# Free-list buffers, a DMA channel and TensorE's pace in a planner's model, and new tables, in an attention, convolution and expert kernel

## The chip, the cores and the metric

The kernel runs on one core of one Trainium2 chip. Its parts are TensorE (PE, matrix products; PEld is its load of stationary operands), VectorE (DVE), ScalarE (ACT), GpSimd (POOL) and SyncE (SP), which only issues transfers here, together with 16 DMA engines. The metric is the device time of one execution in microseconds (us).

## The reference

Three things are computed one after the other. Attention: 8 batches, 8 heads, 256 positions, 64 features per head. Then a gated convolution of 15 taps along the sequence, separately for each of the 512 features, with a silu, added to the attention's output. Then a mixture of experts with two levels of choice (4 groups of 4 experts), where each of the 2048 tokens goes through the one expert that wins.

```python
attn = softmax(q @ k.T / sqrt(D)); x = attn @ v            # B=8 H=8 S=256 D=64, as (B, S, 512)
x_g = x * sigmoid(glu_gate)
conv_out = sum over k of x_g[s + k - 7] * conv_w[:, k]      # 15 taps
x = x + conv_out * sigmoid(conv_out)
g = argmax(x @ w_group); e = argmax(x @ w_expert[g])        # per token
out = softmax weight of g * softmax weight of e * (relu(x @ w1[g, e]) @ w2[g, e])   # 512 -> 1024 -> 512
```

## The kernel before

**Tiles.** A unit `U` is one pair of heads (128 features on the 128 partitions) of two batches; there are 16. Four units, the whole width of 512 features, make a group of two batches (`GS = 2, 2, 2, 2`), and there are four groups. A large operation works on a tile of 128 x 512.

**A unit's way.** `inputs` issues its two loads, qk and gv, on SP's queue. `unit` scales the keys (L327), turns the gate into a tanh (L338) and adds one (t1, L343 or L345). `pair` and `head` do the attention: scores (L362), row maximum on VectorE (`reduce_max`, L390), exponential on ScalarE (L395), transposes on TensorE (L402), a copy pT out of PSUM, the product with v (L381). `tail` builds the reciprocal sums (rb, rc), multiplies (L445, the unit's xT) and gates it (xg, L453). `conv` runs the 15 taps on VectorE (L513, L515), one instruction of 128 x 512 each; for units 2 and 3 (`PC`) `conv_pe` does them as matrix products. Silu and `residual` close the unit; x is split into a high part xh and a low part xl, so that the expert products run in fp32r with three terms.

**A group's way.** `rows` writes the tokens' rows to memory, `route` finds each token's expert (logits at L608, the last step at L697), and picks for each batch the most frequent expert. `loads` and `split` bring that expert's weights in eight pieces of 512 KB (raw) and split each into wh (a cast, L205) and wl (two subtractions of 128 x 512, L731). `dense` runs the batch through it (L758, then L776 to L778), and `store` scales and writes. Tokens with another expert are gathered into three slots (`leftover`, L939 and L963), whose weights come into the gv buffers. A loop at the end takes what still remains; it does not run with these inputs.

**What sets the order.** All instructions are issued in an order that `Flow` plans before the kernel is built. Every step of a generator names an engine, an assumed duration and a key; when the model's engine becomes free, the step with the lowest key among those that are ready goes next. `KEYS` shifts the key of a kind of step, `CD` that of a group's convolutions, and `WAYS` says, one digit for each time, which of the listed engines takes it. Buffers are rings: `get` waits for the oldest one to be returned with `put`. On the chip, each engine runs its instructions in the planned order and waits where data is late. The plan itself costs no time on the chip.

**Start.** `warm` sends `WN` products of zeros through TensorE before the first data is there (L268). SP's queue begins with half of unit 0's qk, the three constants (c_sb with the identity for transposes, the taps cwq, the router's weights wr), and the other half.

## Time and profile before

| | |
|---|---|
| median of 3 runs | 390.2 us (388.56 to 390.43) |
| profiled execution, its own time | 389.96 us |
| its span, first to last instruction | 388.2 us |
| mean granted TensorE clock | 0.974 of 2.4 GHz |
| busy: PE, DVE, POOL, ACT | 359.3, 298.7, 280.7, 224.3 us |

The span is what the profile shows; some 1.8 us of the execution's time lie outside it. A group of instructions is named by its line in the kernel, its engine and its operation. "Idle" and "waited" are times in which an engine stood still until the instruction named after the arrow had ended. The granted clock is 1.00 at 2.4 GHz and 0.50 at 1.2 GHz.

### The profile page before, as it was taken

To read this page: it belongs to the slowest core of one execution; us is meant where nothing else is said; L and a number is where in the kernel's file an instruction comes from. 1 tells how busy PE (TensorE), PEld (TensorE's weight loads), DVE (VectorE), ACT (ScalarE), POOL (GpSimd) and SP (SyncE) were. 2 spreads that over 40 slices of the span, in tenths; PEclk is the share of its full clock that TensorE was granted. 3 is DMA by queue.
4 is the path that set the end of the run, shared out by engine and by line. 5 is a ranking of instruction groups with operands and counts; after the bars stand their busy time and mean duration, and the time that the engine had idled before them with its cause. 6 is when DMAs were issued, how large, how long until landed. Compare 5 with 4: busy or idle time off the path is not lost.

```text
span 388.2 us, 8398 instructions
## 1 busy us (share of the span) xinstructions
PE 359.3 (93%) x2974; PEld 279.6 (72%) x2974; DVE 298.7 (77%) x590; ACT 224.3 (58%) x525; POOL 280.7 (72%) x273
## 2 busy tenths in 40 slices
PE   8898996879999997999999999999799999998993
PEld 7455543658767776877886768878787987986982
DVE  2389989899999999899999999999855541542630
ACT  2888984688858776776878496502443443431210
POOL 4754668299999997899989785877798566376430
PEclk9899999889999998999999999999899999999998
DMA  7523963276617556262643641388858897958301
GB/s 273 218 109 127 253 178 107 86 268 245 214 50 280 209 171 213 114 218 76 221 144 116 205 164 54 117 289 280 301 209 270 302 363 252 345 196 308 110 0 59
DMA packets 27820, 74.88 MB, mean 193 GB/s; under 512 B 2886, under 2 KB 3014, under 8 KB 27776
## 3 DMA queue, kind: packets, MB, share of 16 engines
q1 hardware_dynamic: 24128, 67.79, 51.3%
q10 hardware_dynamic: 3456, 6.29, 4.3%
q8 instruction: 25, 0.41, 0.4%
q0 software_dynamic: 192, 0.24, 0.2%
q14 instruction: 19, 0.16, 0.1%
HBM read 63.67 MB, written 8.59 MB: 186 GB/s over the span
## 4 chain that ended last, share of the span: by engine, by line
PE 43%; DVE 39%; ACT 7%; issue 4%; DMA 3%; POOL 1%; SPq 1%; ACTq 0%; DVEq 0%; POOLq 0%
DVE ac L515 19%; PE sc L758 11%; DVE nm L390 6%; PE mo L776 4%; PE mo L778 4%; PE mo L777 4%; ACT pr L395 3%; PE sc L362 3%; PE av L381 2%; DVE ac L513 2%; PE sc L402 2%; DVE hl L791 2%; PE mo L758 2%; DVE xT L445 2%; PE mo L268 2%
## 5 line engine op out<-in xcount | busy, mean ns | idle before, releaser
L731 POOL TENSOR_TENSOR wl<-raw,wh 128x512 fp32r<-128x512 f32 x117 | 150.4, 1307 | 36.8 <-ACT wh L205 27.0
L515 DVE SCALAR_TENSOR_TENSOR ac<-xg,cwq,ac 128x512 f32<-128x512 f32 x182 | 133.2, 749 | 2.5
L205 ACT CAST wh<-raw 128x1024 fp32r<-128x1024 f32 x54 | 56.7, 1051 | 25.2 <-PE mo L778 20.0
L395 ACT ACTIVATE pr<-sc,nm 128x256 f32<-128x256 f32 x108 | 50.3, 476 | 33.3 <-DVE nm L390 32.9
L776 PE MATMUL mo<-wh,hh 128*128 128x512 f32 x128 | 53.4, 417 | 0.0
L778 PE MATMUL mo<-wh,hl 128*128 128x512 f32 x128 | 50.3, 393 | 0.0
L777 PE MATMUL mo<-wl,hh 128*128 128x512 f32 x128 | 50.1, 391 | 0.0
L402 PE MATMUL sc<-c_sb,pr 128*128 128x128 f32 x216 | 34.3, 288 | 9.9 <-ACT pr L395 9.7
L381 PE MATMUL av<-pT,gv 128*64 128x256 f32 x256 | 38.4, 401 | 3.1 <-ACT pT L205 3.1
L390 DVE TENSOR_REDUCE nm<-sc 128x2 f32<-128x512 f32 x54 | 34.6, 681 | 6.8 <-PE sc L362 6.6
L402 PEld LDWEIGHTS sc<-c_sb,pr 128*128 128x128 f32 x216 | 25.0, 145 | 20.1 <-ACT pr L395 15.3
L362 PE MATMUL sc<-qk 64*128 64x256 f32 x216 | 32.6, 419 | 0.0
L205 ACT COPY pT<-sc 128x512 f32<-128x512 f32 x52 | 30.0, 598 | 4.6 <-PE sc L402 3.8
L453 POOL TENSOR_TENSOR xg<-xT,gv 128x512 f32<-128x512 f32 x16 | 20.9, 1309 | 15.7 <-DVE xT L445 15.6
L776 PEld LDWEIGHTS mo<-wh,hh 128*128 128x128 f32 x128 | 24.0, 188 | 7.9 <-issue 3.2
L381 PEld LDWEIGHTS av<-pT,gv 128*64 128x64 f32 x256 | 17.0, 139 | 16.4 <-ACT pT L205 7.0
L778 PEld LDWEIGHTS mo<-wh,hl 128*128 128x128 f32 x128 | 24.0, 188 | 5.5
L327 POOL TENSOR_SCALAR qk<-qk 128x512 f32<-128x512 f32 (+1 forms) x16 | 23.0, 1439 | 5.7 <-DMA qk<-aQ 5.7
L777 PEld LDWEIGHTS mo<-wl,hh 128*128 128x128 f32 x128 | 24.1, 189 | 4.0
L789 ACT ACTIVATE hh<-sc 128x512 fp32r<-128x512 f32 x18 | 10.8, 598 | 27.1 <-PE sc L758 23.0
L362 PEld LDWEIGHTS sc<-qk 64*128 64x128 f32 x216 | 20.1, 196 | 8.8 <-issue 5.9
L758 PE MATMUL sc<-xT,wh 128*128 128x256 f32 x144 | 24.6, 289 | 0.0
(207 smaller groups left out, 726.2 us busy)
## 6 DMA issues: line engine op xcount, KB each, us to landing
raw<-wE SPq DMA_DIRECT2D x64, 512.0 KB, 4.5
gv<-wE SPq DMA_DIRECT2D x24, 512.0 KB, 5.9
gv<-aG SPq DMA_DIRECT2D x16, 512.0 KB, 5.6
qk<-aQ SPq DMA_DIRECT2D x15, 512.0 KB, 4.6
x_rows<-y ACTq DMA_DIRECT2D x13, 256.0 KB, 2.8
out_dram<-y ACTq DMA_DIRECT2D x11, 256.0 KB, 3.3
out_dram<-y SPq DMA_DIRECT2D x5, 256.0 KB, 5.0
wh<-xg SPq DMA_DIRECT2D x4, 270.0 KB, 4.7
```

Of the source, the lines that this page charges most:

```text
L205: (a_.copy if e == "ACT" else on[e].tensor_copy)(o, i)
L362: t_.matmul(scs[hh][:, qt, :], t[sl, i, qt * P:(qt + 1) * P], t[sl, i, 256:512], start=True, stop=True)
L381: t_.matmul(u.a[64 * hh:64 * hh + 64, i, :], u.vt[:, i, kt, hh, :], pTs[hh][1][:, kt, :], start=kt == 0, stop=kt == 1)
L390: v_.reduce_max(nm[:, hh, :], sc, axis=AX.X, negate=True)
L395: a_.activation(pr[:, qt, :], sc[:, qt, :], AF.Exp, bias=nm[:, hh, qt:qt + 1], scale=1.0, accum_out=u.sm[:, i, qt, hh, 0:1])
L402: t_.transpose(tp[:, kt, qt * P:(qt + 1) * P], pr[:, qt, kt * P:(kt + 1) * P], ident)
L515: v_.scalar_tensor_tensor(acc if k == KT - 1 else ac, x, w, ac, ALU.mult, ALU.add)
L731: on[e].tensor_tensor(wl[:, sl], raw[:, sl], wh[:, sl].bitcast(F32), ALU.subtract)
L758: t_.matmul(hp[:, f, :], ww[:, f, c, :], x, start=k == 0, stop=k == 11)
L776: t_.matmul(ys[t], hh[:, k, sl], w3h[:, k, :], start=j == 0 and k == 0, stop=False)
L777: t_.matmul(ys[t], hh[:, k, sl], w3l[:, k, :], start=False, stop=False)
L778: t_.matmul(ys[t], hl[:, k, sl], w3h[:, k, :], start=False, stop=j == 3 and k == 1)
```

## The change

The buffers that hold xg, xT, xh and xl (16 and 19 in two rings) become 25 slots of one size in a free list: `take` asks for any free slot, `back` returns it. The first use of a slot for xg is asked for behind the gate's tanh, for xT behind the last product with v. xh and xl are returned behind the first layer of the group's last batch. `NQK` goes from 3 to 2 and `HB`, the buffers of the hidden layer, from 4 to 7.

The plan's model changes: `land` is one DMA channel of 400 KB per us with 2.0 us of latency, where SP was held for 0.9 to 1.8 us per load before; an issue now holds SP for 0.45. `pace` stretches TensorE's steps in the model where it has been idle. Some assumed durations are new.

At the start, 36 products of zeros are sent instead of 61, both halves of unit 0's qk are issued first, then c_sb, and cwq and wr only behind unit 1's loads, with a flag `taps` ahead of the convolutions. `UC`, the products of the first expert layer that are planned as one step, goes from 6 to 4. rb may be made on POOL. `CD`, `KEYS` and `WAYS` are new. Where `WAYS` has a 1 for xg, the step t1 falls away and VectorE adds one and multiplies in one instruction.

```diff
--- before.py
+++ after.py
-WN = 61
+WN = 36
...
-N1, N2 = (NC * GS.count(n) for n in (1, 2))
-XS = 0, 3
-HB = 4
-NQK, NGV = 3, 5
+NSL = 25
+HB = 7
+NQK = 2
+NGV = 5
...
-CD = 4.5, 5.37, 11.11, 14.25
+CD = 9.29, 16.05, 17.59, 10.88
...
-UC = 6
+UC = 4
...
-WAYS = dict(rb='0000000000000001', rc='1', xd='0000001000010001', yd='00000001100111', xr='00000000000011', t1='000001111', wh='000000001000000000000000000000000111100000000000000000000101111', ls='01011', pT='00000000000000000000000000010000000000000000000000000000000001', kk='0000000000001', xh='01000000011001', xl='0000000000100001', silu='000000000000012', res='000001000010101', y='000000110111111', wl='0000000000000000000000000000000000000000000000000000000000000000001000000000000000000000000000000000010101010110000001000010101')
-KEYS = dict(tg=-0.45, tp=0.19, rb=1.65, res=1.05, th=-6.86, ls=1.56, conv=1.51, hl=2.4, wh=3.95, t1=1.96, lt=0.08, cp=-2.0, hh=-1.85, max=0.9, sp=-3.29, xr=-1.54, rows=1.63, exp=0.27, dn=0.24, xl=-0.19, rc=0.35)
+WAYS = dict(xg='00000001000101', kk='100100000011', xh='1100010000111011', ls='111', xr='001', yd='000110011', res='0000010000000101', xd='0011001111100011', rc='10001', t1='1101010101100111', wh='000000000001000010000001001010000010000010000101110111', silu='2112220202200011', pT='101100000000000000000000000000000000000000000000000000010011', xl='01010000000101', y='001001000111111', wl='00000001000000000100000000000000000000000000000001010101000100010101000101100000000000011001000000000000111110101111111010000111', rb='2211000000010022')
+KEYS = dict(av=1.39, rt=17.63, max=-6.26, rows=-10.24, cp=7.78, score=0.71, x=-9.24, exp=-0.24, tg=1.23, rb=0.33, ls=4.81, y=-8.67, xg=0.95, t1=0.43, lt=1.85, rc=-3.04, dn=0.11, tp=0.52, res=1.78, pT=0.07, wh=1.78)
...
+    def pool(self, b, n):
+        self.spare[b], self.want[b] = [(0.0, None, i) for i in range(n)], []
+
+    def serve(self, b):
+        while self.want[b] and self.spare[b]:
+            w = min(self.want[b], key=lambda x: x[:2])
+            self.want[b].remove(w)
+            x = min(self.spare[b], key=lambda x: (x[0], x[2]))
+            self.spare[b].remove(x)
+            k = w[2]
+            if x[0] > k[2]:
+                k[2:4] = x[:2]
+            k[4] = x[2]
+            now = self.now
+            self.step(k)
+            self.now = now
+
+    def back(self, b, i):
+        self.spare[b].append((*self.now[2:4], i))
+        self.serve(b)
+
+    def land(self, kb):
+        self.chan = max(self.now[2] + 2.0, self.chan) + kb / 400
+        return self.chan
+
+    def pace(self, t, d):
+        if t >= self.slow:
+            a = max(0.0, t - 4.0)
+            busy = sum(max(0.0, min(y, t) - max(x, a)) for x, y in self.pe[-12:])
+            if t > 5.0 and busy < 2.3:
+                self.slow = t + 4.0
+        if t < self.slow:
+            d = min(2 * d, d + (self.slow - t) / 2)
+        self.pe.append((t, t + d))
+        return d
...
-            k[2], k[3], k[4] = t + x[3], e, e
+            k[2], k[3], k[4] = t + (self.pace(t, x[3]) if e == "PE" else x[3]), e, e
...
-              hb=HB, y=2, rb=1, xg1=N1, xg2=N2, xT1=N1 + XS[0], xT2=N2 + XS[1])
+              hb=HB, y=2, rb=1)
+    fl.pool("sl", NSL)
...
+    def slot(i, dt, u, w=S):
+        return work.tile([P, MB, XW], dt, name=f"sl{i}", bufs=1)[:, 0:u.nb, 0:w]
...
     def setup():
         s_.dma_start(out=c_sb, in_=cst)
+        fl.go(ready1(), KP, fl.land(420))
+
+    def ready1():
+        yield run("DVE", 0.1, 0.5)
+        v_.tensor_copy(rec[:, :, 0], tok1)
+        v_.memset(base, 0.0)
+
+    taps = Flag()
+
+    def ready2():
+        yield run("DVE", 0.15, -1)
+        v_.tensor_scalar(cwq, cwq, 0.25, None, ALU.mult)
+        fl.set(taps)
+
+    def setup2():
         s_.dma_start(out=cwq, in_=cw)
         s_.dma_start(out=wr_sb, in_=wr)
-        v_.tensor_scalar(cwq, cwq, 0.25, None, ALU.mult)
-        v_.tensor_copy(rec[:, :, 0], tok1)
-        v_.memset(base, 0.0)
+        fl.go(ready2(), KP, fl.land(1000))
...
     def inputs():
-        for u in us:
-            u.ng = yield get(f"xg{u.nb}")
-            u.xg = work.tile([P, u.nb, XW], F32, name=f"xg{u.nb}", bufs=fl.bufs[f"xg{u.nb}"])
-            u.nx = yield get(f"xT{u.nb}")
-            u.xT = work.tile([P, u.nb, S], F32, name=f"xT{u.nb}", bufs=fl.bufs[f"xT{u.nb}"])
         for u in us:
             u.iq = yield get("qk")
             u.qk = inp.tile([P, MB, 512], F32, name="qk", bufs=NQK)
             if u.n == 0:
                 u.half = []
                 for i in range(u.nb):
-                    yield run("SP", 1.0)
+                    yield run("SP", 0.45)
                     s_.dma_start(out=u.qk[:, i], in_=aQ[u.b + i, u.p])
-                    u.half.append(fl.now[2] + 2.0)
-                    if i == 0:
-                        setup()
+                    u.half.append(fl.land(256))
+                yield run("SP", 0.45)
+                setup()
             else:
-                yield run("SP", 0.9 * u.nb)
+                yield run("SP", 0.45)
                 s_.dma_start(out=u.qk[:, 0:u.nb], in_=aQ[u.b:u.b + u.nb, u.p].rearrange("b p f -> p b f"))
-            qt = fl.now[2] + 2.0
+                qt = fl.land(256 * u.nb)
             u.iv = yield get("gv")
             u.gv = inp.tile([P, MB, 512], F32, name="gv", bufs=NGV)
-            yield run("SP", 0.9 * u.nb)
+            yield run("SP", 0.45)
             s_.dma_start(out=u.gv[:, 0:u.nb], in_=aG[u.b:u.b + u.nb, u.p].rearrange("b p f -> p b f"))
-            u.tv = fl.now[2] + 2.0
+            u.tv = fl.land(256 * u.nb)
             fl.go(unit(u), u.k, qt if u.n else u.half[0])
+            if u.n == 1:
+                yield run("SP", 0.9)
+                setup2()
...
-            e = yield at("t1", u.n, KP, ("POOL", 0.1 + 0.57 * nb), ("ACT", 0.1 + 0.21 * nb))
+            e = yield at("t1", u.n, KP, ("POOL", 0.49 * nb), ("ACT", 0.1 + 0.21 * nb))
             if e == "POOL":
                 g_.tensor_tensor(tg, tg, ones[:, 0:1].unsqueeze(1).broadcast_to([P, nb, 256]), ALU.add)
             else:
                 a_.activation(tg, tg, AF.Copy, bias=1.0)
         fl.set(u.gate)
-        yield run("POOL", 0.2, KP)
+        u.ng = yield take("sl")
+        u.xg = slot(u.ng, F32, u, XW)
+        yield run("POOL", 0.11, KP)
         g_.memset(u.xg[:, :, 0:PAD], 0.0)
         g_.memset(u.xg[:, :, S + PAD:], 0.0)
+        fl.set(u.pad)
...
-        e = yield at("rb", u.n, u.k, ("ACT", 0.1 + 0.21 * nb), ("DVE", 0.12 + 0.24 * nb))
+        e = yield at("rb", u.n, u.k, ("ACT", 0.1 + 0.21 * nb), ("DVE", 0.07 + 0.14 * nb), ("POOL", 0.5 * nb))
...
+        u.nx = yield take("sl")
+        u.xT = slot(u.nx, F32, u)
         yield at("x", 0, u.k, ("DVE", 0.08 + 0.265 * nb))
         v_.tensor_tensor(u.xT[:, 0:nb], u.a[:, 0:nb], rb[:, 0:nb], ALU.mult)
...
+        yield flag(u.pad)
...
-        yield run("SP", 1.6, -20)
+        yield run("SP", 2.4, -20)
...
-        yield sleep(3.0, "SP")
+        fl.now[2] = max(fl.now[2] + 3.2, fl.land(1200))
...
+        yield flag(taps)
...
-            yield run("POOL", 0.1 + 0.57 * nb, -3)
+            yield run("POOL", 0.1 + 0.61 * nb, -3)
...
+        fl.back("sl", u.ng)
         fl.set(u.x)
-        yield get(f"xg{nb}")
-        u.xh = work.tile([P, nb, XW], F32R, name=f"xg{nb}", bufs=fl.bufs[f"xg{nb}"])[:, :, 0:S]
+        u.nh = yield take("sl")
+        u.xh = slot(u.nh, F32R, u)
         e = yield at("xh", u.n, -2, ("ACT", 0.1 + 0.21 * nb), ("DVE", 0.1 + 0.14 * nb))
         copy(e, u.xh, x)
-        yield get(f"xT{nb}")
-        u.xl = work.tile([P, nb, S], F32R, name=f"xT{nb}", bufs=fl.bufs[f"xT{nb}"])
+        u.nl = yield take("sl")
+        u.xl = slot(u.nl, F32R, u)
...
+        fl.back("sl", u.nx)
...
-        w = yield at("xd", 2 * b + t, -1, ("ACT", 0.43), ("SP", 0.9))
+        w = yield at("xd", 2 * b + t, -1, ("ACT", 0.43), ("SP", 0.45))
         on[w].dma_start(out=x_tok[(2 * b + t) * P:(2 * b + t + 1) * P, :], in_=xr)
-        yield sleep(2.5)
+        fl.now[2] = fl.land(256)
...
-        e = yield at("wh", 8 * m.b + n, -1, ("ACT", 0.95), ("DVE", 0.65))
+        e = yield at("wh", 8 * m.b + n, -1, ("ACT", 0.95), ("DVE", 0.8))
...
+            if m.i == gr[m.g].nb - 1:
+                for u in xs:
+                    fl.back("sl", u.nh)
+                    fl.back("sl", u.nl)
...
-        yield run("DVE", 4.5)
+        yield run("DVE", 5.5)
...
-                yield run("SP", 1.8)
-                fl.go(split(m, n, ir, fetch(gr[m.g].es[m.i], n)), -1, fl.now[2] + 2.3)
+                yield run("SP", 0.45)
+                raw = fetch(gr[m.g].es[m.i], n)
+                fl.go(split(m, n, ir, raw), -1, fl.land(512))
...
-                yield run("SP", 1.8)
+                yield run("SP", 0.45)
                 s_.dma_start(out=w, in_=wE[bass.ds(e, 1), j].rearrange("a p f -> p (a f)"))
-                ls_[s].w[j] = ii, w, fl.now[2] + 2.3
+                ls_[s].w[j] = ii, w, fl.land(512)
```

## Rows read from the trace of the kernel before

**Rows 1.** The page's first part: busy time of each engine, its share of the span, and its instructions.
```profile
PE 359.3 (93%) x2974; PEld 279.6 (72%) x2974; DVE 298.7 (77%) x590; ACT 224.3 (58%) x525; POOL 280.7 (72%) x273
```

**Rows 2.** The span cut into six stages: from and to, length, then busy time (instructions) of PE, PEld, DVE, ACT and POOL, granted clock, mean share of the DMA engines, GB/s.
```profile
0.00:7.00 7.00, 5.99 (x63) 5.89 (x63) 1.15 (x3) 1.28 (x1) 2.55 (x9) 1.00 0.71 238
7.00:80.00 73.00, 62.38 (x431) 36.51 (x430) 59.86 (x115) 55.69 (x161) 43.99 (x61) 0.95 0.50 161
80.00:285.00 205.00, 195.20 (x1545) 155.84 (x1546) 195.82 (x377) 136.26 (x320) 176.97 (x161) 0.98 0.54 186
285.00:331.40 46.40, 46.40 (x555) 38.57 (x553) 20.45 (x72) 18.75 (x27) 32.74 (x26) 1.00 0.87 300
331.40:380.60 49.20, 48.17 (x385) 42.20 (x383) 20.84 (x26) 11.63 (x18) 24.41 (x19) 1.00 0.51 181
380.60:388.20 7.60, 1.11 (x5) 0.56 (x3) 0.53 (x1) 0.69 (x1) 0.00 (x0) 0.79 0.21 75
```

**Rows 3.** Who waited for whom over the whole span: us in all, times, longest.
```profile
ACT pr L395 <- DVE nm L390: 33.7, 20, 6.8
```

**Rows 4.** The same for the first 90 us.
```profile
ACT pr L395 <- DVE nm L390: 13.1, 7, 6.8
...
PE sc L402 <- ACT pr L395: 7.4, 6, 2.9
```

**Rows 5.** The same from 90 to 285 us.
```profile
PE sc L402 <- ACT pr L395: 2.4, 3, 1.8
```

**Rows 6.** Groups of instructions over the whole span: line, engine, operation, out<-in, shapes, count | busy us, mean ns of one | idle before them and what ended it.
```profile
L515 DVE SCALAR_TENSOR_TENSOR ac<-xg,cwq,ac 128x512 f32<-128x512 f32 x182 | 133.2, 749 | 2.5
L390 DVE TENSOR_REDUCE nm<-sc 128x2 f32<-128x512 f32 x54 | 34.6, 681 | 6.8 <-PE sc L362 6.6
L395 ACT ACTIVATE pr<-sc,nm 128x256 f32<-128x256 f32 x108 | 50.3, 476 | 33.3 <-DVE nm L390 32.9 <-DVE mo L633 0.4
L205 ACT COPY pT<-sc 128x512 f32<-128x512 f32 x52 | 30.0, 598 | 4.6 <-PE sc L402 3.8 <-ACT y L803 0.7
L731 POOL TENSOR_TENSOR wl<-raw,wh 128x512 fp32r<-128x512 f32 x117 | 150.4, 1307 | 36.8 <-ACT wh L205 27.0 <-DVE wh L205 4.5 <-PE sc L758 2.0
L731 DVE TENSOR_TENSOR wl<-raw,wh 128x512 fp32r<-128x512 f32 x11 | 11.7, 1065 | 12.0 <-ACT wh L205 11.7
L558 DVE TENSOR_TENSOR xT<-xT,xg 128x512 fp32r<-128x512 f32 x2 | 1.4, 677 | 0.0
L205 ACT CAST wh<-raw 128x1024 fp32r<-128x1024 f32 x54 | 56.7, 1051 | 25.2 <-PE mo L778 20.0 <-DVE emx L632 3.9 <-POOL xT L528 0.5
L343 POOL TENSOR_TENSOR gv<-gv,c_sb 128x512 f32<-128x512 f32 x12 | 12.5, 1038 | 9.5 <-ACT gv L338 9.5
L268 PE MATMUL mo<-wz 128*128 128x128 bf16 x61 | 6.0, 294 | 1.0 <-POOL sm L320 1.0
```

**Rows 7.** The instructions of L445 alone, which end a unit's attention, in two stages: from and to, length, VectorE's busy time in them (how many), clock, DMA share, GB/s.
```profile
20.00:40.00 20.00, 1.74 (x3) 1.00 0.39 138
60.00:90.00 30.00, 0.69 (x1) 0.89 0.52 184
```

**Rows 8.** The time line of the first 25 us, in pieces: start, us, engine, line, operation, out<-in, count, idle before. The row at 1.73 is a stretch of the zeros in the row at 1.01.
```profile
1.01 6.04 PE L268 MATMUL mo<-wz 128*128 128x128 bf16 x61 [1.01 <-POOL sm L320]
1.73 1.49 PE L268 MATMUL mo<-wz 128*128 128x128 bf16 x12
2.62 0.43 SPq L301 DMA_DIRECT2D qk<-aQ  x1
3.33 0.86 POOL L327 TENSOR_SCALAR qk<-qk 128x256 f32<-128x256 f32 x1 [2.33 <-DMA qk<-aQ]
6.80 0.85 POOL L327 TENSOR_SCALAR qk<-qk 128x256 f32<-128x256 f32 x1 [0.96 <-DMA qk<-aQ]
6.98 1.14 PE L362 MATMUL sc<-qk 64*128 64x256 f32 x8
13.61 1.98 PE L381 MATMUL av<-pT,gv 128*64 128x256 f32 x8
18.19 1.08 PE L381 MATMUL av<-pT,gv 128*64 128x256 f32 x8
21.83 0.75 DVE L513 TENSOR_SCALAR ac<-xg,cwq 128x512 f32<-128x512 f32 x1 [0.17 <-POOL xg L453]
```

**Rows 9.** Two single microseconds as stages, columns as in Rows 2.
```profile
13.00:14.00 1.00, 1.00 (x6) 0.57 (x6) 0.00 (x0) 1.00 (x6) 1.00 (x1) 0.51 1.03 393
18.00:19.00 1.00, 1.00 (x11) 0.51 (x9) 1.00 (x3) 0.58 (x3) 1.00 (x4) 1.00 0.00 0
```

**Rows 10.** Transfers by issue: out<-in, queue, count, KB each, median us from issue to landing.
```profile
raw<-wE SPq DMA_DIRECT2D x64, 512.0 KB, 4.5
gv<-wE SPq DMA_DIRECT2D x24, 512.0 KB, 5.9
...
qk<-aQ SPq DMA_DIRECT2D x15, 512.0 KB, 4.6
...
cwq<-cw SPq DMA_DIRECT2D x1, 30.0 KB, 3.2
```

**Rows 11.** The time line around the last group, in pieces: its last tap, the last step of its routing, the first product of its first expert layer.
```profile
284.54 0.74 DVE L515 SCALAR_TENSOR_TENSOR acc<-xg,cwq,ac 128x512 f32<-128x512 f32 x1
...
305.11 0.18 DVE L697 RECIPROCAL rec<-sg 128x4 f32<-128x4 f32 x1
...
331.35 0.38 PE L758 MATMUL sc<-xg,wh 128*128 128x256 f32 x1
```

19 lines of the change are left out of this document (13 added, 6 removed).

## The prediction

> **What bounds the kernel now.** I read the page's busy totals first, then the span cut into stages, then who waited for whom, and last the time lines of the two ends. TensorE is busy for 359.3 of 388.2 us [rows 1], so a shorter span has to come out of the remaining 28.9 us, out of the time at a lower clock, or out of less TensorE work. The stages [rows 2] say where they are. TensorE stands still for 1.0 us before 7 us, for 73.0 - 62.4 = 10.6 us from 7 to 80, for 205.0 - 195.2 = 9.8 us from 80 to 285, for nothing from 285 to 331.4, for 1.0 us until its last matmul, and for 6.5 us in the tail. VectorE is busy for 195.8 of the 205 us of the middle stage and for less than half of the time behind it. So two engines share the bound up to 285 us, and TensorE has it alone behind that.
>
> What TensorE waits for in the first stages is seen in the waits: for 7.4 us in the first 90 it waited [rows 4] to transpose probabilities until an exponential was done. One step further back, ScalarE's exponentials waited 33.7 us over the span for the row maximum on VectorE [rows 3], 13.1 of them in the first 90 us. VectorE takes its work in the written order, and the taps of the convolution (182 of 749 ns [rows 6]) stand ahead of the maximum. The cadence agrees: three units finish attention (L445) from 20 to 40 us, one from 60 to 90 [rows 7].
>
> **The change part by part.** The sum is made against the profiled execution: span 388.2, its own time 389.96 (1.8 around the span), the median of the three runs 390.2, which is 0.2 above.
>
> *Zeros.* Twelve of them take 1.49 us, the last one 0.29 of that, so 0.109 us from one to the next [rows 6, 8]; the 36 that stay end at 1.01 + 35 x 0.109 + 0.29 = 5.1 us. The first score now starts at 6.98. Its keys are there earlier: scaling began at 3.33 on POOL and takes 0.86 [rows 8]. So the first score moves by -1.9 us. Against it, the granted clock: the zeros ran at the lower pace up to about 6, and eight matmuls of one form took 1.98 us where the granted clock was 0.51 (1.2 GHz) and 1.08 where it was full (2.4 GHz) [rows 8, 9]. One group of eight at the lower clock gives back 0.9. I take -1.0; bounds -1.9 and +0.8 (three groups of eight at the lower clock). The Trainium skill ("TensorE: Matmul & The Clock Gate", section on the HAM clock gate) says that the array starts throttled, that activity lifts this and idling brings it back. That speaks against fewer zeros; by it the head would be worth the +0.8 end of my bounds, not -1.0.
>
> *Order of the first transfers.* The second half of qk is issued at 2.62 behind three constants; without their issues of 0.43 us it goes out 1.3 us earlier, and its scaling, which waited for it until 6.80, can start at 5.5, in time for TensorE, which is then at the first half [rows 8]. The taps' weights cwq and wr go behind two units' loads. They are covered: the first tap runs at 21.83 [rows 8], and this load took 3.2 us [rows 10]. Without that cover each microsecond by which they land later than the first tap would be a microsecond on VectorE. Costed at nothing.
>
> *Order on the engines (the new KEYS and CD).* This is the large part. A maximum gets the key u.k - 6.26 (before u.k + 0.9), the product L445 u.k - 9.24, and the taps u.k + 9.29 to 17.59 (before, with KEYS, 6.0 to 15.8). So VectorE takes a maximum whenever one is ready and fills up with taps. Of the 7.4 us in the first 90 I take 5.5 as regained (the first unit's chain, which no order shortens, keeps the rest); bounds 0 and the stage's whole 10.6. From 90 to 285 the same wait is 2.4 us [rows 5]; I take all 2.4, bounds 0 and 9.8. What could be late next is group 0's convolution, pushed back by attention. A unit's four maxima of 0.68 take 2.7 us on VectorE, while its eight exponentials of 0.48 and four copies of 0.60 take 6.2 us on ScalarE [rows 6]; VectorE has about half of its time for taps, so I take nothing there. UC 6 to 4 and HB 4 to 7 only loosen the order; costed within these terms.
>
> *Clock.* The stage 7 to 80 has a mean clock of 0.95 and the next 0.98 [rows 2], together 7.3 + 8.2 = about 15 us at low clock, about half of it lost. With fewer holes I take one of these drops away: -1.7, half of one drop of 3.4 us; bounds 0 and -7.
>
> *Work moved between engines.* Counted from the tables. 22 more wl halves go from POOL (1307 ns) to VectorE (1065, or 677 as for the same form in L558) [rows 6]: POOL -28.8, VectorE +14.9 to +23.4. wh: four more on VectorE, four of 1051 ns fewer on ScalarE, -4.2. silu: 9 fewer POOL operations, at wl's price -11.8; 5 more on ScalarE, 2 on VectorE. t1: 7 fewer on POOL (1038), 4 more on ScalarE. xg in one step on VectorE three times, kk three more times there, pT four, xh four, xl two, rb two; rb four times on POOL, which no row shows: between nothing and wl's 1.3 us each, taken as t1's 1.04, off the path. The counts by engine, small ones at the price of their nearest row: POOL about -54, ScalarE about -8, VectorE +30 to +40. POOL and ScalarE are not the bound. VectorE is, until its last tap: by the batch numbers about 23 us of the addition stand ahead of it, the rest falls to batches 4 to 7, where VectorE is 44% busy [rows 2]. The last tap ends at 285.3, group 3's routing at 305.3, and its first matmul runs at 331.35 [rows 11]. So 26 us of TensorE's backlog hide a later convolution; the idle VectorE of the first 7 us (5.9 us [rows 2]) is partly filled as well. Cost +1.0; bounds 0 and +4. Without that cover it is one for one.
>
> *Buffers.* 35 buffers of x become 25 slots, qk has two in place of three. A finished group holds 8 slots (xh, xl) until its second batch is through, a unit under way 2. That leaves room for about eight units beside one finished group, more than the five that the gv buffers admit. A qk buffer has two units' time, at least twice ScalarE's 6.2 us, for a load of 4.6 [rows 10] and a scaling (0.86 for a half [rows 8]). Nothing.
>
> *Tail.* Behind 380.6 the order is the same: matmul, scaling, store. Nothing.
>
> Sum: -1.0 - 5.5 - 2.4 - 1.7 + 1.0 = -9.6. Span 378.6, own time 380.4, median about 380.5.
>
> **The rivals.**
> A. *VectorE's additions take the gain back.* If the last tap moves by 23 us and the dense work of group 3 waits for it, its first matmul comes at about 331 and not 10 us earlier. For it: VectorE is 96% busy before 285 us. Against it: the 26 us of cover. Time: only the head's -1.0 is left, 389.
>
> B. *Transfers later than planned (the other side).* The new plan lets a load of 512 KB land 2.0 + 512/400 = 3.3 us after the channel is free, and counts 0.45 us of issue; the rows say 4.5 (raw), 4.6 (qk), 5.9 (gv) from issue to landing [rows 10]. The order is fixed ahead, so an instruction that is early in a queue for late data stops all behind it: ScalarE's wh cast in front of an exponential is the place. A late load costs 1.2 us; of 64 loads of raw, 12 on the path cost 14.4, which gives 380.5 + 14.4 = 395. Eight loads decide the sign. For it: 87% of the channel in use from 285 to 331 [rows 2]. Against it: 393 GB/s were moved at 13 us [rows 9], so the pace of the plan exists. The Trainium skill ("DMA: Bandwidth & Descriptors", anatomy of one DMA) gives about 2.0 us fixed and the rest by size, close to the plan; the rows here are 1.2 to 2.6 us longer, and the rows decide.
>
> C. *The tables change the order but nothing on the path*: 390, within 0.5%.
>
> **How the numbers follow.** About 0.5% (2 us) is what a measurement of this kernel can tell. Forecast, faster: 0.66, its own range 368 (all 20.4 us of holes from 7 to 285 and 1.9 of the head regained) to 388. Rivals A and C together 0.16, at 388.3 to 392.1; A's 389 lies in it. Rival B, and additions to VectorE beyond its cover, 0.18, at 392.2 to 400. The range 368 to 393 leaves out some 0.17 above and 0.03 below. The point is the forecast's.
>
> **What would show it.** First score near 5.1 us. ScalarE's wait for the maximum well under 33.7 us, TensorE's for the exponential in the first 90 under 4. TensorE's idle time from 7 to 80 near 5 us. More than one L445 from 60 to 90. VectorE busy 330 to 338, POOL near 227, ScalarE near 216. Group 3's routing may end later than 305.3, and the first matmul behind it should come near 322. I am wrong if the waits for the maximum stay, if TensorE idles before group 3's first matmul with routing as the releaser (A), or if casts and scalings wait for DMA (B).

## The result, and the profile after

The changed kernel takes 393.7 us (median), the kernel before 390.05 beside it; the ratio is 1.0133, 95% interval 1.0100 to 1.0167. By the ratio it is slower by 1.3% (by the medians 0.9%), where 380.5 us were forecast; it lies 0.7 us above the upper end of the range. Ratios compare undisturbed executions alone and medians take in all of them (two of the changed kernel's 20 took 566 and 670 us); executions of one kernel lie up to 11 us apart (383.65 to 394.91 for the kernel before in one series), so the two can differ by half a per cent or more, and only what both show is built on. The profiled execution took 393.09 us with a span of 391.2, 3.0 more than before. The engines' sums on its page came out close to the forecast:

```profile
...
PE 359.2 (92%) x2949; PEld 279.7 (71%) x2949; DVE 330.9 (85%) x637; ACT 219.5 (56%) x515; POOL 233.8 (60%) x231
```

Three of the six stages of [rows 2] in the changed kernel (columns: stretch and its length, busy us of PE, PEld, DVE, ACT and POOL with their instructions, mean granted clock, DMA share, GB/s):

```profile
...
7.00:80.00 73.00, 61.80 (x434) 36.21 (x430) 63.29 (x121) 52.45 (x157) 32.56 (x50) 0.94 0.45 143
80.00:285.00 205.00, 195.69 (x1544) 155.90 (x1545) 197.91 (x385) 135.09 (x311) 151.74 (x141) 0.96 0.55 195
285.00:331.40 46.40, 43.20 (x527) 36.12 (x528) 36.67 (x77) 13.42 (x23) 23.73 (x19) 0.96 0.76 262
```

TensorE stands still for 73.0 - 61.8 = 11.2 us from 7 to 80 (10.6 before) and for 9.3 from 80 to 285 (9.8 before): the two stages that were to give 7.9 us gave nothing. The clock, 0.95 and 0.98 before, is 0.94 and 0.96. From 285 to 331.4, where TensorE had no hole before, it now has 3.2 us. The waits over the whole span (total, times, longest):

```profile
...
ACT pr L460 <- DVE nm L455: 27.3, 25, 3.4
...
ACT wh L252 <- DMA raw<-wE: 22.0, 10, 4.5
...
PE sc L467 <- ACT pr L460: 9.8, 8, 4.1
```

ScalarE's wait for the maximum fell from 33.7 [rows 3] to 27.3 us. TensorE's wait for the exponential stayed at 9.8 (9.7 before). And a new wait has come: 22.0 us of wh casts on ScalarE that stand still for raw, where no such wait is to be seen before. In the first 90 us, for which [rows 4] has 13.1 and 7.4:

```profile
...
PE sc L467 <- ACT pr L460: 8.1, 4, 4.1
ACT wh L252 <- DMA raw<-wE: 6.8, 3, 4.5
ACT pr L460 <- DVE nm L455: 5.9, 9, 1.2
...
PE mo L467 <- ACT pr L460: 2.2, 3, 1.1
```

The second form of TensorE's wait, in the kernel before:

```profile
...
PE mo L402 <- ACT pr L395: 0.7, 1, 0.7
```

TensorE waits longer for its exponentials there than before (8.1 and 2.2 us for the two forms, 7.4 and 0.7 before). The wait for the maximum is down by 7.2 us, but 6.8 us of waiting for raw have come in the same queue, and a wait is put down to what ended last. In f1, a run below in which batch 0's first pieces are loaded early, the wait for raw is gone from the first 90 us, and ScalarE's wait for the maximum over the whole span is back at its old figure:

```profile
...
ACT pr L460 <- DVE nm L455: 33.6, 27, 4.7
```

So the maxima had not come earlier. The starts and ends in the two traces say the same: the second maximum of a pair of heads starts 1.1 us after the pair's scores have ended in the kernel before and 1.4 us in the changed one (means of 32 pairs; 0.6 us of it is the first maximum of the pair).

A finer cut shows where time went and came from; first the kernel before, then the changed one:

```profile
...
7.00:90.00 83.00, 70.73 (x482) 42.36 (x482) 68.79 (x135) 65.00 (x183) 53.18 (x68) 0.94 0.55 182
...
66.00:100.00 34.00, 29.16 (x202) 21.51 (x203) 30.89 (x72) 27.71 (x66) 25.29 (x24) 0.90 0.55 196
...
90.00:285.00 195.00, 186.84 (x1496) 149.99 (x1495) 186.89 (x357) 126.95 (x296) 167.77 (x154) 0.98 0.52 178
...
285.00:312.00 27.00, 27.00 (x348) 22.95 (x347) 14.20 (x62) 11.03 (x17) 19.99 (x17) 1.00 0.87 298
```

```profile
...
7.00:90.00 83.00, 66.70 (x453) 39.88 (x449) 72.88 (x142) 56.62 (x165) 36.78 (x54) 0.89 0.49 159
...
66.00:100.00 34.00, 24.67 (x151) 18.05 (x148) 30.85 (x73) 19.98 (x47) 18.10 (x19) 0.75 0.51 182
...
90.00:285.00 195.00, 190.79 (x1524) 152.23 (x1525) 188.32 (x364) 130.91 (x304) 147.52 (x138) 0.99 0.54 191
...
285.00:312.00 27.00, 24.44 (x366) 20.81 (x363) 25.25 (x41) 8.91 (x14) 19.26 (x15) 0.94 0.84 295
```

Idle time of TensorE in the changed kernel less that before: +4.0 us from 7 to 90, -4.0 from 90 to 285, +3.2 from 285 to 331.4, and -0.3 behind 331.4. That makes +3.0 from the exact figures, the 3.0 of the span. So the change does win 4.0 us, between 90 and 285. It loses as much before 90 (from 66 to 100 alone the idle time is 4.5 us longer, with a granted clock of 0.75 on top), and 3.2 behind 285. TensorE's busy time is level (359.2 and 359.3 us), although the zeros take 2.0 us less (4.02 in place of 6.04); the rest of its work took 1.9 us longer.

### The profile page after: what moved, and what is told of

Its sections match the earlier page's. It is cut to its first block, busy times and chain, and to the rows that moved or that the text cites. A ratio compares the mean times of both kernels' runs of the same rounds, so it can differ in the third digit from the quotient of the medians.

```text
span 391.2 us, 8315 instructions
## 1 busy us (share of the span) xinstructions
PE 359.2 (92%) x2949; PEld 279.7 (71%) x2949; DVE 330.9 (85%) x637; ACT 219.5 (56%) x515; POOL 233.8 (60%) x231
## 4 chain that ended last, share of the span: by engine, by line
DVE 41%; PE 34%; DMA 12%; POOL 4%; issue 4%; ACT 2%; SPq 1%; POOLq 0%; DVEq 0%; ACTq 0%
DVE ac L584 14%; PE sc L827 9%; DVE nm L455 6%; DMA raw<-wE 5%; DMA xs<-x_rows,ix 3%; PE mo L849 3%; PE mo L851 3%; PE mo L850 3%; PE mo L827 3%; POOL wl L800 3%; PE sc L467 3%; PE av L446 2%; DMA qk<-aQ 2%; PE sc L427 2%; DVE sl L512 2%
## 5 line engine op out<-in xcount | busy, mean ns | idle before, releaser
L800 POOL TENSOR_TENSOR wl<-raw,wh 128x512 fp32r<-128x512 f32 x95 | 126.4, 1348 | 67.2 <-ACT wh L252 45.4
L584 DVE SCALAR_TENSOR_TENSOR ac<-sl,cwq,ac 128x512 f32<-128x512 f32 x182 | 130.5, 748 | 1.5
L252 ACT CAST wh<-raw 128x1024 fp32r<-128x1024 f32 x50 | 52.4, 1048 | 38.0 <-DMA raw<-wE 22.0
L467 PE MATMUL sc<-c_sb,pr 128*128 128x128 f32 x216 | 34.9, 290 | 10.0 <-ACT pr L460 9.8
L827 PE MATMUL sc<-sl,wh 128*128 128x256 f32 x288 | 42.3, 289 | 0.0
L467 PEld LDWEIGHTS sc<-c_sb,pr 128*128 128x128 f32 x216 | 25.1, 146 | 20.3 <-ACT pr L460 16.6
L827 PEld LDWEIGHTS sc<-sl,wh 128*128 128x128 f32 x288 | 37.7, 192 | 1.6 <-issue 1.2
L800 DVE TENSOR_TENSOR wl<-raw,wh 128x512 fp32r<-128x512 f32 x33 | 29.6, 924 | 7.8 <-ACT wh L252 7.6
L827 PE MATMUL mo<-sl,wh 128*128 128x256 f32 x224 | 34.9, 294 | 1.0 <-ACT wh L252 1.0
L427 PE MATMUL sc<-qk 64*128 64x256 f32 x216 | 34.4, 442 | 0.0
L827 PEld LDWEIGHTS mo<-sl,wh 128*128 128x128 f32 x224 | 29.7, 193 | 3.4 <-ACT wh L252 1.7
L521 POOL TENSOR_TENSOR sl<-sl,gv 128x512 f32<-128x512 f32 x13 | 17.3, 1328 | 22.1 <-DVE sl L512 22.1
```

Of the source, the lines that this page charges most:

```text
L252: (a_.copy if e == "ACT" else on[e].tensor_copy)(o, i)
L427: t_.matmul(scs[hh][:, qt, :], t[sl, i, qt * P:(qt + 1) * P], t[sl, i, 256:512], start=True, stop=True)
L467: t_.transpose(tp[:, kt, qt * P:(qt + 1) * P], pr[:, qt, kt * P:(kt + 1) * P], ident)
L584: v_.scalar_tensor_tensor(acc if k == KT - 1 else ac, x, w, ac, ALU.mult, ALU.add)
L800: on[e].tensor_tensor(wl[:, sl], raw[:, sl], wh[:, sl].bitcast(F32), ALU.subtract)
L827: t_.matmul(hp[:, f, :], ww[:, f, c, :], x, start=k == 0, stop=k == 11)
```

## The experiments

In all of them the planned order on the engines is left as it is in the kernel named, unless the text says otherwise. Medians and ratios are taken as in the result; a2's ratio rests on two executions, hence its wide interval.

| run | built on | median, and that of before beside it | ratio (95%) |
|---|---|---|---|
| the change | | 393.71, 390.05 | 1.0133 (1.0100 to 1.0167) |
| a1_half_raw | changed | 389.76, 388.58 | 1.0020 (0.9990 to 1.0050) |
| b1_half_raw | before | 386.80, 388.58 | 0.9962 (0.9933 to 0.9992) |
| a2_wl_pool | changed | 393.56, 388.58 | 1.0148 (1.0075 to 1.0221) |
| a3_zeros61 | changed | 392.58, 388.58 | 1.0081 (1.0033 to 1.0129) |
| a4_half_all | changed | 389.85, 389.71 | 0.9990 (0.9949 to 1.0030) |
| b2_half_all | before | 386.75, 389.71 | 0.9894 (0.9831 to 0.9957) |
| b3_zeros36 | before | 386.95, 389.71 | 0.9970 (0.9932 to 1.0009) |
| b4_head | before | 388.98, 389.71 | 1.0055 (1.0009 to 1.0101) |
| d1_g3_taps | changed | 393.18, 389.36 | 1.0165 (1.0128 to 1.0202) |
| d2_more_taps | before | 416.38, 389.36 | 1.0638 (1.0566 to 1.0711) |
| d3_taps_half | changed | 387.90, 389.36 | 0.9996 (0.9961 to 1.0031) |
| d4_old_first | changed | 391.88, 389.36 | 1.0079 (1.0046 to 1.0112) |
| f1_early_raw | changed | 392.80, 388.59 | 1.0086 (1.0044 to 1.0127) |
| f2_no_gather_wait | changed | 393.16, 388.59 | 1.0133 (1.0089 to 1.0176) |
| f3_all_three | changed | 391.37, 388.59 | 1.0045 (1.0007 to 1.0082) |
| f4_zeros24 | before | 388.03, 388.59 | 0.9991 (0.9962 to 1.0020) |
| g1_taps_gather | changed | 391.27, 388.53 | 1.0073 (1.0035 to 1.0111) |
| g2_all_four | changed | 390.30, 388.53 | 1.0051 (1.0017 to 1.0084) |

### Are the transfers to blame? Pieces of half size in both kernels

a1 and b1 load only the first half of each expert piece and use it twice; a4 and b2 do so for the leftover slots' pieces too.

```diff
-        s_.dma_start(out=raw, in_=wE[bass.ds(e, 1), j].rearrange("a p f -> p (a f)"))
+        s_.dma_start(out=raw[:, 0:w], in_=wE[bass.ds(e, 1), j].rearrange("a p f -> p (a f)")[:, 0:w])
...
-        copy(e, wh, raw)
+        copy(e, wh.rearrange("p (a f) -> p a f", a=2), raw[:, 0:DM].unsqueeze(1).broadcast_to([P, 2, DM]))
...
```

> The changed kernel with every expert piece loaded only half (256 KB in place of 512; both halves of a piece are then built from its first half, so half of the expert weights are left out). The order on every engine stays the same. Transfer theory (casts on ScalarE wait 22.0 us for raw): that wait falls under 5 us and the time falls by 6 to 10, to 384 to 388. VectorE theory (its added work puts the last tap 28 us later, and group 3 behind it): the last tap stays within 2 us of 313 and the time stays within 2 us of 393.7; only what the transfers cost VectorE comes back.

> The kernel before with the same edit (half of the expert weights left out). Its casts do not wait for raw in its profile, so both theories expect 388 to 390, at most 2 us less than before. If it gains as much as the changed kernel does, the transfers are no cause of the difference.

> The changed kernel with the expert pieces (raw) and the pieces of the three leftover slots (gv from wE) loaded only half; half of the expert weights are left out. Order unchanged. With raw alone halved it stood at 1.002 of the kernel before, from 1.0133. Transfer theory: the leftover loads share the channel with raw behind 245 us, so the rest of the loss goes too, 0.990 to 0.998. Order theory (the new order itself is no better and loses time where no transfer is late): 1.000 to 1.003, at most 0.2% less than with raw alone.

> The kernel before with the same edit, as the control (raw alone: 0.9962). Transfer theory: 0.993 to 0.997, that is, little more to gain, so that the two kernels come within 0.3% of each other once the transfers are short. Order theory: the same figure, but the changed kernel stays 0.5% or more above it.

The casts' wait for raw fell from 22.0 to 8.8 us in a1. By the ratios the changed kernel gained 1.1 points with a1 and 1.4 with a4, but the kernel before gained 0.4 and 1.1 with the same edits; by the medians it is 0.6 and 0.9 against 0.5 and 0.8. With all pieces half, the distance between the two is still 1.0 point (0.9990 against 0.9894; 0.8 by the medians). So transfers cost time in both kernels; late ones account for no more than some 0.4 to 0.8 of the 1.3 points by the ratios, and for 0.1 to 0.2 of 0.9 by the medians.

### Is VectorE's load to blame?

a2 puts 16 wl subtractions of batches 0 to 5 back on POOL. d1 leaves out every second tap of group 3. d2 gives the kernel before 27 us more of taps. d3 is a4 with d1's edit.

```diff
 a2
-            on[e].tensor_tensor(wl[:, sl], raw[:, sl], wh[:, sl].bitcast(F32), ALU.subtract)
+            (on[e] if m.b > 5 else g_).tensor_tensor(wl[:, sl], raw[:, sl], wh[:, sl].bitcast(F32), ALU.subtract)
 d1, in the loop over the taps
+                if u.g == GA and k % 2:
+                    continue
 d2, behind a tap
+                if u.g == GA and 1 <= k <= 9:
+                    v_.scalar_tensor_tensor(ac, x, w, ac, ALU.mult, ALU.add)
```

> The changed kernel with the 16 wl subtractions of batches 0 to 5 that it puts on VectorE given back to POOL, every other instruction in its order. VectorE theory: 13.3 us leave VectorE ahead of the last tap, the last tap comes 10 to 13 us earlier (300 to 304), group 3 stops being late, and the time falls by 3 to 6, to 388 to 391. Transfer theory: no change, 393 to 394.5.

> The changed kernel, order untouched, with every second tap of group 3's convolution left out (28 VectorE instructions of some 0.75 us, 21 us). Theory 'late group 3': the cover of 26 us is overdrawn by 26.4 us of lateness; with the last tap near 291 in place of 311.7, the gap before group 3's first matmul closes, TensorE no longer idles from 285 to 331, and the time falls by 3 to 4.5 us, to 389 to 390.5 (ratio to before near 1.002). Rival 'hidden anyway, the loss is the transfers': last tap moves as much, time within 1 us of the changed kernel's 393.7.

> The kernel before, order untouched, with taps 1 to 9 of group 3's convolution done twice (36 more VectorE instructions, 27 us, so the output is another one); the last tap should move from 285.3 to about 312, where the changed kernel has it. Theory 'late group 3': routing 26 us later, first matmul of group 3 (331.3) 2 to 5 us later, time 2 to 5 us longer than before (ratio 1.005 to 1.013). Rival 'the cover holds it': ratio within 1.000 +- 0.003.

> The changed kernel with both edits: all expert pieces loaded half (the other half of the weights left out) and every second tap of group 3 left out. If late transfers and the late group 3 are two separate costs they add up: 393.7 - 3.9 (all pieces half, as measured) - 3 to 4 (taps) = 386 to 387, ratio to before near 0.99, as the kernel before has it with half pieces (0.9894). If both are one cost, it stays at 389 to 390.

In the changed kernel the last tap ends at 311.7 us, 26.4 later than before:

```profile
...
303.09 0.28 DVE L991 COPY xsT<-av 128x128 f32<-128x128 f32 x1
...
310.96 0.75 DVE L584 SCALAR_TENSOR_TENSOR acc<-sl,cwq,ac 128x512 f32<-128x512 f32 x1
```

With 8.6 us less of VectorE's work up to it (a2) it ended only 3.3 us earlier, and with 14.9 us less (d1) again only 3.3, and these two profiled executions were as a whole 3.7 and 3.0 us shorter than the changed kernel's. Taps stand in VectorE's queue between a copy of gathered rows (L991 above) and other steps that wait for data. Neither run gave time back. d3, with half pieces as well, lies 2 us under a4 by the medians and level with it by the ratios (0.9996 and 0.9990). So the lateness of group 3's convolution is a matter of place in the queue more than of VectorE's sum; the whole addition was not taken away in any run.

d2 is the clearest miss of a theory. 27 us more of taps in the kernel before cost 25 to 27 us, where at most 5 were expected. The stretch 80 to 240 us, before and then d2:

```profile
...
80.00:240.00 160.00, 153.72 (x1049) 119.08 (x1050) 152.95 (x297) 120.94 (x298) 143.38 (x134) 0.98 0.51 178
```

```profile
...
80.00:240.00 160.00, 142.87 (x938) 110.34 (x938) 153.66 (x269) 110.84 (x266) 134.38 (x127) 0.94 0.50 169
```

TensorE's idle time there grows from 6.3 to 17.1 us: 18 of the 36 extra taps stand in the queue before 240 us, ahead of group 2's last attention and routing (its logits start at 240.2 in place of 225.5). The 26 us between group 3's routing and its first product cover only what nothing else queues behind.

### The head

b3 sends 36 products of zeros in the kernel before, f4 24, a3 61 in the changed one. b4 is b3 with the whole new order of first loads; d4 is the changed kernel with the old order of first loads.

```diff
 d4
-        s_.dma_start(out=c_sb, in_=cst)
...
-        s_.dma_start(out=cwq, in_=cw)
-        s_.dma_start(out=wr_sb, in_=wr)
...
                     u.half.append(fl.land(256))
+                    if i == 0:
+                        s_.dma_start(out=c_sb, in_=cst)
+                        s_.dma_start(out=cwq, in_=cw)
+                        s_.dma_start(out=wr_sb, in_=wr)
```

> The changed kernel with 61 products of zeros again. The prediction's step gave 36 a gain of 1.0 us at the head. If the head reaches the end, 394.7; if VectorE sets the end, TensorE's head is covered and the time stays within 1 us of 393.7. If the clock of the first units matters more than the wait, it is below 393.

> The kernel before with 36 products of zeros in place of 61 and nothing else. The prediction's step: TensorE free 1.9 us earlier, 0.9 lost to the lower clock, 0.997. But half of unit 0's keys is scaled only at 7.65 there, so only the first group of scores moves: between 0.997 and 1.000. If the first units at the lower clock cost more than the wait, 1.002 to 1.006.

> The kernel before with the whole new head: 36 products of zeros, both halves of qk ahead of the constants, cwq and wr behind unit 1's loads, the scaling of the taps ahead of the first tap. Everything behind is in the old order. If the head is worth what the prediction said (1.0 us) and reaches the end: 0.997. If the queue of the first loads and the clock eat it: 0.999 to 1.004.

> The changed kernel, order on the engines untouched, with the first loads issued as before: the three constants between the two halves of qk, none behind unit 1. If the new order of first loads costs what it cost in the kernel before (0.85 points there), the time falls by 1 to 3 us to 390.5 to 392.5. If the cost there came from POOL's preparation of the taps standing between the two scalings, which the changed kernel may have elsewhere, the time stays at 393.7 or rises by up to 1.5 (second score later by 1.3).

> The kernel before with 24 matmuls of zeros in place of 61, nothing else. With 36 it took 0.7 per cent less by the medians (386.95 against 389.71) and the first score came at 4.8 us. If the zeros are the limit of the first score, it comes at 3.8 to 4.3 and the time is 1 us less again; if its keys are (first half scaled at about 4.2) or the clock falls behind them, nothing more is gained: 387 to 388.5.

Fewer zeros alone bring the first score to 4.8 us in the kernel before; what that is worth is not clear of noise (0.3% by the ratio with an interval to 1.0009, 0.7% by the medians), and 24 show no more. In the changed kernel they give nothing: 61 zeros (a3) were not slower than its 36, and the first transposes start at 10.91 us with 61 and at 10.86 with 36. The new order of first loads costs 0.85 points in the kernel before (b4 against b3; 0.5 by the medians) and some 0.5 in the changed one (the change against d4; 0.3 by the medians, and the two intervals overlap). In b4 POOL waits for c_sb to prepare the taps (L469) with the second half's scaling behind it, and TensorE waits 2.9 us for keys (2.2 in b3): its second score starts at 9.63 us, at 8.07 in b3. The waits of the first 14 us in b4:

```profile
...
POOL wd L469 <- DMA c_sb<-cst: 3.3, 1, 3.3
...
PE mo L366 <- POOL qk L331: 2.9, 1, 2.9
```

In the changed kernel the second score is early, but ScalarE's queue has unit 0's tanh of gv ahead of the first exponential, and gv is late: it is issued 1.0 us earlier than in d4 (at 2.14, there at 3.10), and its tanh starts 0.8 us later (start, duration; in brackets the idle time before). The changed kernel, then d4:

```profile
...
8.60 0.63 ACT L400 ACTIVATE gv<-gv 128x512 f32<-128x512 f32 x1 [6.57 <-DMA gv<-aG]
...
9.80 0.46 ACT L460 ACTIVATE pr<-sc,nm 128x256 f32<-128x256 f32 x1
...
10.86 2.03 PE L467 MATMUL sc<-c_sb,pr 128*128 128x128 f32 x8 [2.92 <-ACT pr L460]
```

```profile
...
7.82 0.63 ACT L401 ACTIVATE gv<-gv 128x512 f32<-128x512 f32 x1 [5.77 <-DMA gv<-aG]
...
9.01 0.46 ACT L461 ACTIVATE pr<-sc,nm 128x256 f32<-128x256 f32 x1
```

The first maximum was there at about 7.8 us. The exponential starts at 9.80, and at 9.01 with the old order. TensorE stands still for 2.92 us meanwhile (1.64 in d4), and the granted clock is lower behind it. The stretch from 12 to 18 us of the changed kernel and of d4:

```profile
...
12.00:18.00 6.00, 6.00 (x29) 3.88 (x28) 2.91 (x7) 5.09 (x19) 1.41 (x3) 0.57 0.21 76
```

```profile
...
12.00:18.00 6.00, 6.00 (x40) 4.09 (x38) 2.82 (x6) 5.33 (x20) 2.11 (x3) 0.76 0.12 44
```

### The two stretches with the losses

From 66 to 100 us. TensorE in the changed kernel, with the scores (L427), a step of group 0's routing (L733) and the transposes that wait for exponentials (L467), and then the scores in the kernel before:

```profile
...
65.31 1.14 PE L427 MATMUL sc<-qk 64*128 64x256 f32 x8
...
76.86 0.63 PE L733 MATMUL mo<-oh,c_sb 128*128 128x32 f32 x4 [1.56 <-DVE oh L727]
...
81.54 2.08 PE L427 MATMUL sc<-qk 64*128 64x256 f32 x8
...
89.94 1.12 PE L467 MATMUL sc<-c_sb,pr 128*128 128x128 f32 x4 [4.08 <-ACT pr L460]
```

```profile
...
62.68 1.13 PE L362 MATMUL sc<-qk 64*128 64x256 f32 x8
...
76.07 1.13 PE L362 MATMUL sc<-qk 64*128 64x256 f32 x8
...
82.57 2.08 PE L362 MATMUL sc<-qk 64*128 64x256 f32 x8
```

The changed kernel issues no score between 65.3 and 81.5 us; before, they came at 62.7, 76.1, 82.6 and 88.5, between the steps of the routing. TensorE stands still twice for the routing's VectorE steps (1.56 us, and 0.90 at L750) with no attention to fill in. VectorE starts no maximum between 69.3 and 85.1 us, although its key is low. The scores that began at 81.54 ended at 83.6; VectorE, at work without a pause, had taps and the last nine steps of the routing ahead of their maximum, and reached it behind the last of them:

```profile
...
84.99 0.18 DVE L766 RECIPROCAL rec<-sg 128x4 f32<-128x4 f32 x1
85.09 1.26 DVE L455 TENSOR_REDUCE nm<-sc 128x2 f32<-128x512 f32 x2
```

ScalarE then has casts, which wait for raw, between the exponentials:

```profile
...
88.38 1.04 ACT L252 CAST wh<-raw 128x1024 fp32r<-128x1024 f32 x1 [1.61 <-DMA raw<-wE]
89.33 0.47 ACT L460 ACTIVATE pr<-sc,nm 128x256 f32<-128x256 f32 x1
```

f1 takes these waits for raw away: batch 0's first four pieces come from a fixed expert and are issued before the routing has ended. f2 does the like for the stretch behind 285 us: the transposes of the gathered rows read a constant. f3 is f1, f2 and d4 together; g1 is f2 with d1's edit, g2 all four.

```diff
 f1, ahead of the reading of the expert's number
+        if G_.g == 0:
+            for j in range(NRAW):
+                raw = wraw.tile([P, CW], F32, name="raw")
+                s_.dma_start(out=raw, in_=wE[0:1, j].rearrange("a p f -> p (a f)"))
+                early.append(raw)
...
-                raw = fetch(gr[m.g].es[m.i], n)
+                raw = early.pop(0) if early else fetch(gr[m.g].es[m.i], n)
...
 f2
-        t_.transpose(xp[:, 0:P], xs, ident)
+        t_.transpose(xp[:, 0:P], ident, ident)
```

> The changed kernel with the first four expert pieces of batch 0 taken from expert 0 (so batch 0's output is another one), issued before SyncE reads the chosen expert's number; order on the engines untouched. Theory 'casts that wait for raw hold ScalarE's exponentials at 83 to 90 us': the 4.08 us wait of TensorE for the exponential at 89.94 falls to near 1, the stretch at half clock (78.7 to 95.7) gets shorter, the time falls by 2 to 4 us to 390 to 392. Rival 'attention was held back by the order anyway (the maxima stand behind the routing of group 0 until 85.1)': the casts come earlier, the exponentials at 86.2 do not, time within 1 us of 393.7.

> The changed kernel with the transposes of the gathered rows reading a constant in place of them (so the leftover slots' output is another one); the gathers still run. Theory 'the loss from 290 to 310 is the gather that lands after 7.0 us, 4.6 planned': the waits of 3.3 us for it and the drop of the clock at 300.5 go, time down by 2.5 to 4.5 us, to 389 to 391. Rival 'group 3's late convolution and routing': batch 6 starts at 333 to 335 all the same, time within 1 us of 393.7.

> The changed kernel with both edits and the first loads issued as in the kernel before. If the three are separate costs: 393.7 less 1.8 (first loads, as measured) less what the two others give (5 to 8), 385 to 388, below the kernel before; then the order itself gains a few us and late transfers at three places take them back. If the order itself gained nothing, 389 to 391, the kernel before's own time.

> The changed kernel with both edits for the stretch 285 to 312 us: every second tap of group 3 left out, and the transposes of the gathered rows reading a constant (so group 3's convolution and the leftover slots' output are others). One edit alone brought nothing; without the gather's wait (2.6 us) TensorE waited 2.8 us at the next instruction, for a copy of these rows that stands behind taps in VectorE's queue, and without the taps it waited 2.3 us for the gather. Theory 'two causes end at the same place': with both gone the wait goes, and the time falls by 2.5 to 4 us, to 389.5 to 391. Rival 'VectorE's written order waits on TensorE itself, so that nothing is won there': within 1 us of 393.

> As the kernel with three edits (fixed expert for batch 0's first four pieces, loaded before the routing has ended; constant in place of the gathered rows; first loads as in the kernel before; 391.4 measured), and every second tap of group 3 left out. If the cost at 285 to 312 is real and needs both edits: 387 to 389, level with the kernel before. If it stays at 391, the new order is slower by some 2.5 us with none of its suspected waits left, and the rest is in the attention that it starves around group 0's routing (70 to 90 us).

f1: the rival holds, mostly. Without the late pieces TensorE still waits 3.03 us for the exponential, and ScalarE waits 4.7 us for the maximum, which stands behind the routing on VectorE as before. g2 tells the score from the maximum. Its scores end at 79.7 us, 3.9 earlier than in the changed kernel, and its routing is 1.9 earlier; its maximum comes 1.9 earlier, behind the routing again, and TensorE's wait is longer. f1, then g2:

```profile
...
81.93 2.08 PE L427 MATMUL sc<-qk 64*128 64x256 f32 x8
...
88.20 0.65 PE L467 MATMUL sc<-c_sb,pr 128*128 128x128 f32 x4 [3.03 <-ACT pr L460]
```

```profile
...
78.60 1.13 PE L428 MATMUL sc<-qk 64*128 64x256 f32 x8
...
83.09 0.18 DVE L769 RECIPROCAL rec<-sg 128x4 f32<-128x4 f32 x1
83.18 1.26 DVE L456 TENSOR_REDUCE nm<-sc 128x2 f32<-128x512 f32 x2
...
85.89 1.12 PE L468 MATMUL sc<-c_sb,pr 128*128 128x128 f32 x4 [5.49 <-ACT pr L461]
```

So from 79.7 to 83.2 us in g2 it is the order on VectorE that holds attention up, with the scores there. f1's time is within the spread of the changed kernel's own (ratio 0.5 points lower, the quotient of the medians not).

Behind 285 us the one wait of TensorE has several causes, each of which ends just behind the other. The changed kernel, f2, d1 and g1:

```profile
...
PE av L988 <- DMA xs<-x_rows,ix: 2.6, 1, 2.6
```

```profile
...
PE av L1012 <- DVE xsT L991: 2.8, 1, 2.8
```

```profile
...
PE av L990 <- DMA xs<-x_rows,ix: 2.3, 1, 2.3
```

```profile
...
PE av L1014 <- DVE xsT L993: 2.5, 1, 2.5
```

The rows that a transfer gathers land late (the plan has 4.6 us):

```profile
...
DMA to landing us min/median/max: 4.2/6.5/7.0
```

Without that wait (f2), TensorE waits 2.8 us one instruction later, for a copy of the rows that VectorE reaches at 303.65 us, behind taps and wl. Without half of the taps (d1) it waits 2.3 us for the gather. Without either (g1) it still waits 2.5 for the copy, now behind a cast of 1.50 and two wl of 3.01 us together. Each alone gave no time; together they gave 0.2 to 0.6 points (g1), and beside the other two edits nothing by the ratios (1.0051 in g2, 1.0045 in f3), all at the edge of what these runs can tell.

f3 was to take 385 to 388 us if its three costs were separate, and took 391.4. With all four edits (g2) the kernel is still 0.5% slower than before (1.0017 to 1.0084). The waits have not gone with the edits: TensorE still waits 2.5 us for the copy, and from 66 to 100 us it stands still for 8.8 us, 4.8 before. g2:

```profile
...
66.00:100.00 34.00, 25.16 (x177) 19.85 (x177) 32.46 (x75) 22.50 (x52) 19.86 (x21) 0.90 0.38 125
```

By the traces the largest part that is left lies there, in the place that the order gives to scores and maxima around group 0's routing. That is read and not tried: no run puts them back between the routing's steps, since each edit of a key moves the whole order, and the work moved to VectorE and the smaller buffers stay in every run on the changed kernel.

No run is clearly faster than both kernels with the output unchanged. The kernel before with 36 zeros comes nearest (0.9970, to 1.0009).

## Why the prediction was wrong

*Zeros: -1.0.* The first score came at 4.96 us (5.1 forecast). The gain is lost within 6 us: the first transposes start at 10.86, before at 10.46, since what came next on the path was the exponential behind a late load. In the kernel before (b3) the first score moves as well, and what it is worth there is not clear of noise. The clock, which was only a bound of this term, came in another place: 0.57 from 12 to 18 us, behind a hole of 2.92. The Trainium skill ("TensorE: Matmul & The Clock Gate", section on HAM oscillation) says that holes while waiting for data bring the low clock back; the trace agrees, 0.50 from 78.7 to 95.7 as well, behind a stretch from 70 to 78 us in which TensorE was at work for 5.6 of 8.

*Order of first transfers: nothing.* Wrong by 0.3 to 0.5 points (d4), 0.5 to 0.85 in the kernel before (b4). The argument followed the second half of qk alone. It did not ask what else would land late: c_sb, for which POOL's wd waits 3.3 us in b4 with the keys behind it, and gv, for which the changed kernel's tanh waits 6.6, with exponentials behind it.

*Order on the engines: -5.5 and -2.4.* This is the step that failed, and by most. From 90 to 285 us TensorE's idle time fell by 4.0 us, more than the 2.4; from 7 to 90 it rose by 4.0, where 5.5 were to be gained. The step was read from a chain of two waits, TensorE for the exponential, the exponential for the maximum. It took the second wait for lateness of VectorE's maxima behind taps, and a low key for the cure. But the maxima were hardly late: before, the second of a pair starts 1.1 us behind the pair's scores, and 0.6 of that is the first. What ScalarE waited for was mostly the score. Nor did the key bring the maxima closer (1.4 us), and around group 0's routing, where the first 90 us lose most, they stand behind taps and the routing's last steps. The fall of the second wait by 7.2 us was a change in what ScalarE's idle time is put down to. What sets the cadence there is the place of attention in both queues: scores on TensorE and maxima on VectorE came between the routing's steps before, and come behind them now. The sign "more than one L445 from 60 to 90" came true without a gain: units finish attention at 63.1, 71.7 and 98.3 us in the changed kernel between 55 and 100, and before at 56.6, 75.1 and 95.4. The forecast read the keys of VectorE's steps and not that of the rows' transposes (`rows` from 1.63 to -10.24). That these transposes hold the banks that scores need is likely from the code, and was not shown.

*Clock: -1.7.* It went the other way, 0.963 from 0.974 over the span. By the stretches shown, 2 x (1 - 0.94) x 83 = 10 us of the time from 7 to 90 were at the lower clock before, and 18 are now. The 3.4 us that the term takes for one drop stand in no row ahead of it; the trace of the kernel before has such a stretch at 0.52, from 67.5 to 70.8 us.

*Work moved to VectorE: +1.0 under a cover of 26 us.* The sum of busy time (330.9) was right; some 30 us, not 23, stood ahead of the last tap (287.0 us busy up to it, 257.1 before). The tap moved by 26.4 us, the end of group 3's routing by 24.8, and group 3's first product by 3.3, to 334.6. So in the changed kernel the cover held for the routing, and the term lies within its bounds: from 285 us to the first product TensorE stood still for 3.2 us, 2.6 of them for the gathered rows (with the copy behind taps close behind, f2) and 0.6 for the residual of group 3. d2 shows that such a cover cannot be counted on: as much work as this, put into the kernel before, cost 25 to 27 us, since half of it came ahead of group 2. Rival A gave about 331 for the first product, and 334.6 was measured, but its sign is not there: TensorE did not stand still with the routing as releaser. Taking part of VectorE's work away (a2, d1) brought the product back by 3.2 and 2.5 us, no more than these executions were shorter as a whole.

*Rival B* gave 395 and named the place, wh casts ahead of exponentials. The mechanism is there (22.0 us of casts waiting, and late data twice more, at the head and at the gather), but its price is not: 14.4 us of path were put on it, and taking the waits away gives some 0.5 points or less at each place (f1, d4, f2). Its band, 392.2 to 400, holds the result by luck: the number was near, the share of the causes was wrong.

*Buffers, tail: nothing.* No row shows a wait for a slot, a qk buffer or a bank among the large ones of TensorE; nothing speaks against these terms. They were not tried alone.

## What to carry to other kernels

A wait two steps back is not the bound, and it is put down only to what ended last: before a chain of waits is turned into a gain, compare the start of each step with the end of the one that feeds it (1.1 us a pair here, where the wait showed 33.7 in all), look at what else could end last at each link, and whether there is work in the queue ahead to fill the hole. Where several things end within a microsecond or two of each other, taking one away gives nothing, and a sum of single gains is not to be had. A cover lasts only for what has nothing else in the same queue behind it; doubling the work in the kernel before (d2) would have shown this in one run.
